# Gate stage of a fused attention and MoE kernel: the planner holds operand pieces back on VectorE and ScalarE while a PSUM bank's reading is due

## The chip, the cores and the metric

One NeuronCore of a Trainium2 chip runs the whole program. The metric is the device time of one execution in microseconds (us). The engines are TensorE (PE; its weight loads are listed as PEld), VectorE (DVE), ScalarE (ACT), GpSimd (POOL) and SyncE (SP), which here issues all DMAs. Each engine works through its own list of instructions in the order in which the program was written, and waits on semaphores where an instruction needs what another engine has made, or a buffer that another engine still reads.

## What is computed

The reference, cut to what matters:

```python
def reference(q, k, v, n_sink, window, w1, w2, w3, wo, w_in, w_out, g_ln):
    a = softmax(mask(q @ k.T / 8))            # 4 x 8 heads, 768 positions, 4 sinks, window 128
    x = (a @ v) as 3072 tokens x 512
    h = ((x @ w1) * (x @ w2)) @ w3 @ wo       # the gate is the product of the first two
    h = h @ w_in                              # 512 -> 1024
    s = h * softmax(h)
    return layer_norm(s) * g_ln @ w_out       # 3072 x 512, float32
```

## The kernel before

After attention, the rest of the program is one list of tasks. The function `op` (line 925) notes for each task its engine, an expected duration in ns, a rank, the step to run and the sets of places that it reads and writes. `arrange` (line 49) then plans the lists: it keeps a clock for each engine, puts every task whose predecessors are placed into `wait[engine]` with the time at which it becomes ready, moves it to `go[engine]` once the engine's clock has come to that time, and takes from `go` the task with the lowest rank. A rank is roughly the time in ns at which the task is wanted. An engine is free again `OVER` ns before a task ends (82 for DVE, 95 for ACT), a result of TensorE is ready for others 400 ns after its end (`PE_NS`), one of another engine after 232 ns. The order in which tasks are taken becomes the order of the program; the clock itself leaves no trace on the chip.

The gate computes a = x @ w1 and b = x @ w2 and multiplies them. Both matrix products are done as 2 x 2 block products with seven multiplications in place of eight (Strassen's scheme in Winograd's form). There are four batches (`order`, line 988), four groups of columns `m` in each, and 14 products in each group: seven (`k`) for w1 (`z` = 0) and seven for w2 (`z` = 1), in the order

```python
both = [(1, 0), (1, 1), (2, 0), (6, 0), (2, 1), (6, 1), (5, 0), (7, 0),
        (5, 1), (7, 1), (4, 0), (3, 0), (4, 1), (3, 1)]
```

A product (`product`, line 974) is six matmuls of 128x128 by 128x384, since every operand is split into a high and a low part (high by high, high by low, low by high, for two blocks of rows). It is planned with MM = 1041 ns. It is written into one PSUM bank of six, X, Y and Z for each `z` (line 971): bank index 3 z + BANK[k]. The eight banks are allocated as four tiles of two banks (`four_banks`, line 888): tile 0 holds X and Y of z = 0, tile 1 holds Z of z = 0 and X of z = 1, tile 2 holds Y and Z of z = 1. So (2,0) and (6,0) write into the same tile, and so do (2,1) and (5,0), (4,1) and (3,1), and (1,1) after (3,1).

The results are read from the banks by two kinds of instructions, the readings. A ScalarE copy (`copy`, line 940, recorded at line 158) reads Y after k = 1, 6, 7 and, for z = 0, after 4. A VectorE addition or multiplication (`two`, line 946, recorded at line 948) reads X after k = 2, Z after k = 7 and k = 3, and, for z = 1, Y after k = 4. VectorE then multiplies the two halves' results, `p_[0]*p_[1]` after (2,1), `u3[0]*u3[1]` after (7,1), `u2[0]*u2[1]` after (3,1), from SBUF to SBUF (line 948 as well), and SP sends each to DRAM (`abd`).

On the same two engines run the pieces that make operands. `parts_of` (line 952) makes the factors of a block: sums (line 368), high parts (ScalarE, line 158) and low parts (VectorE, line 365, into `hold` for x or into g). They make the factors of the next batch's x at the end of each batch, of w1's and w2's later groups in the first batch, and of the folded w3 @ wo in the last. `convert` (line 1010) turns float64 weights into float32: two ScalarE pieces, `w_sign` (VectorE, line 342), `w_high` (VectorE, line 351) and `w_c` (POOL, line 359). `ns_of` (line 162) gives a piece's planned time: for DVE 140 + 1.055 ns for each column, so 545 ns for 384 columns and 680 for 512.

After the gate come the second product (56 products of 24 matmuls, MM = 2082), the hidden layer with the norm, and the last product, all in the same task list. Their tasks on VectorE and ScalarE, such as the split of `w_in` and the first operands of the second product (`prep`), may be placed while the gate still runs.

The edit touches `RANK`, `arrange` and `op`; it works on the order of the tasks of `parts_of`, `convert`, `two` and `copy` in the gate.

Of the kernel before, what the change touches and what calls it, by code (L numbers as in the profile page):

```python
# [26 lines left out]
    mask=62.62, load=22.12, scores=-355.79, max=-67.26, exp=-12.34, total=-62.48, norm=40.89, T=-21.59,  # L27
    stay=29.46, R_T=-100.61, sink_T=-182.3, T_copy=-50.24, sink_copy=-116.03, V=51.95, out=-62.87, w_load=18.71,
    w_a=-69.73, w_b=67.42, w_c=24.26, w_hi=47.52, w_lo=3.94, fold=163.21, fold_out=40.78, parts=-92.47,
    spill=-105.5, x_parts=71.86, later=-5.34, stage=0.0,  # L30
)
WO_AT, WO_BY, W3_AT, W3_BY, W12_AT, W12_BY = -4.0, 3.0, 21.0, 3.4, 30.0, 12.0
OWN_NS, OTHER_NS, PE_NS = 19, 232, 400

OVER = dict(DVE=82, ACT=95, POOL=45)

PART_OF = dict(scores="rows", V="columns")
SWITCH = {("all", "rows"): 95, ("all", "columns"): 95, ("columns", "all"): 100, ("columns", "rows"): 100}
# [10 lines left out]
def arrange(tasks, ranks=None):  # L49


    ranks = RANK if ranks is None else ranks
    rank = [t[2] + ranks[t[3]] for t in tasks]
    last_w, readers = {}, {}
    before, follow = [0] * len(tasks), [[] for _ in tasks]
    for n, (eng, ns, s, key, f, args, r, w, after) in enumerate(tasks):
        pre = set()
        for x in r:
            if x in last_w:
                pre.add(last_w[x])  # L60
            readers.setdefault(x, []).append(n)
        for x in w:
            if x in last_w:
                pre.add(last_w[x])
            pre.update(m for m in readers.pop(x, ()) if m != n)
            last_w[x] = n
        pre.discard(n)
        before[n] = len(pre)
        for m in pre:
            follow[m].append(n)  # L70
    engine = [t[0].rstrip("+") for t in tasks]
    free = {e: 0 for e in engine}
    if "mask" in (t[3] for t in tasks):
        free["DVE"] = 4000
    port = 0
    kind = "all"
    stay = ranks.get("stay", 0.0)
    at_ns = [0] * len(tasks)
    wait, go = {e: [] for e in free}, {e: [] for e in free}
    for n, e in enumerate(engine):  # L80
        if not before[n]:
            heapq.heappush(wait[e], (0, n))
    order = []
    while len(order) < len(tasks):
        start, eng = min(
            (free[e] if go[e] else max(free[e], wait[e][0][0]), e) for e in free if go[e] or wait[e]
        )
        while wait[eng] and wait[eng][0][0] <= start:
            n = heapq.heappop(wait[eng])[1]
            heapq.heappush(go[eng], (rank[n], n))  # L90
        n = heapq.heappop(go[eng])[1]
        change = 0
        if eng == "PE":
            heapq.heappush(go[eng], (rank[n], n))
            to = {x: PART_OF.get(tasks[x[1]][3], "all") for x in go[eng]}
            x = min(go[eng], key=lambda x: (x[0] + stay * ((kind, to[x]) in SWITCH), x[1]))
            go[eng].remove(x)
            heapq.heapify(go[eng])
            n, change, kind = x[1], SWITCH.get((kind, to[x]), 0), to[x]
        if tasks[n][0][-1] == "+" and port > start:  # L100
            others = [x for x in go[eng] if tasks[x[1]][0][-1] != "+"]
            if others:
                heapq.heappush(go[eng], (rank[n], n))
                go[eng].remove(min(others))
                heapq.heapify(go[eng])
                n = min(others)[1]
            else:
                start = port
        order.append(n)
        end = start + tasks[n][1] + change  # L110
        free[eng] = max(start, end - OVER.get(eng, 0))
        if tasks[n][0][-1] == "+":
            port = free[eng]
        for m in follow[n]:
            lag = OWN_NS if engine[m] == eng else PE_NS if eng == "PE" else OTHER_NS
            at_ns[m] = max(at_ns[m], end + tasks[n][8] + lag)
            before[m] -= 1
            if not before[m]:
                heapq.heappush(wait[engine[m]], (at_ns[m], m))
    return order  # L120
# [3 lines left out]
def attention_moe_kernel(  # L124
# [27 lines left out]
    PE, DVE, ACT, POOL, SP = nc.tensor, nc.vector, nc.scalar, nc.gpsimd, nc.sync  # L152
# [24 lines left out]
    def path(stack, banded):  # L177
# [292 lines left out]
        def x_factors(b):  # L470
            x = x_t[b]
            blk = [x[:, 2 * k:2 * k + 2, S // 2 * n:S // 2 * (n + 1)] for n in range(2) for k in range(2)]
            return factors("right", blk, lambda n: (xop[:, xlie[n], 0], xop[:, xlie[n], 1]))
# [90 lines left out]
        if banded:  # L564
# [143 lines left out]
            tasks = []  # L708
# [155 lines left out]
        else:  # L864
            general_fold()
            general_attention()
            for n in range(4):
                w, m = ("w1", "w2")[n % 2], n // 2
# [20 lines left out]
        banks = {t.tensor.name for t in four_banks}  # L889
        bank = [t[:, i] for t in four_banks for i in range(2)]  # L890
# [14 lines left out]
        def toks(ap):  # L905

            name = ap.tensor.name
            if name not in grain:
                return [name]
            g = grain[name]  # L910
            if g >= P * 384:
                end = ap.offset + sum(d[0] * (d[1] - 1) for d in ap.ap)
                return {(name, x) for x in range(ap.offset // g, end // g + 1)}
            starts = [ap.offset]
            dims = [d for d in ap.ap[1:] if d[0] and d[1] > 1]
            run = 1
            if dims and dims[-1][0] == 1:
                run = dims.pop()[1]
            for stride, n in dims:
                starts = [o + stride * i for o in starts for i in range(n)]  # L920
            return {(name, x) for o in starts for x in range(o // g, (o + run - 1) // g + 1)}

        tasks = []

        def op(eng, ns, rank, outs, ins, f, *args, after=0, both=False, then=None):

            r = set().union(*(toks(a) for a in ins)) if ins else set()
            w = set().union(*(toks(a) for a in outs))
            if then is not None:
                r.add(then)  # L930
            tasks.append((eng + "+" * (eng == "POOL" or both), ns, rank, "stage", f, args, r - w, w, after))

        def dma(rank, out, in_, then=None):

# [17 lines left out]
        def parts_of(steps, cols, rank, sums="POOL", lows="DVE"):  # L952

            for kind, n, outs, ins, args in steps:
                eng = "ACT" if kind == "hi" else sums if kind == "sum" else lows[n % len(lows)] if isinstance(lows, tuple) else lows
                k = 1
                for d in outs[0].shape[1:]:
                    k *= d

                many = outs[0].shape[1]  # L960
                by = max(1, many * 512 // k) if len(outs[0].shape) > 2 else many
                for i in range(0, many, by):
                    w, r, a = ([x[:, i:i + by] if hasattr(x, "shape") else x for x in l] for l in (outs, ins, args))
                    op(eng, ns_of(eng, k * by // many), rank(n, kind), w, r, do_step, kind, engines[eng], a, both=eng == "DVE")
# [19 lines left out]
        both = [(1, 0), (1, 1), (2, 0), (6, 0), (2, 1), (6, 1), (5, 0), (7, 0), (5, 1), (7, 1), (4, 0), (3, 0), (4, 1), (3, 1)]  # L984
# [38 lines left out]
        op("SP", 475, 50000, [g_sb], [], lambda: SP.dma_start(out=g_sb, in_=g_ln.rearrange("(c p) -> p c", p=P)), after=3000)  # L1023
        MM = 1041
        later = [("win", f) for f in range(8)] + [("wout", f) for f in range(8)]
        wpiece = [slots[0][:, 4 * i * KB:4 * (i + 1) * KB] for i in range(3)]
        wfop = [t[:, 14 * KB * i:14 * KB * (i + 1)].rearrange("p (s u n) -> p s u n", s=7, u=2) for t in groups[:2] for i in range(2)]
        for bi, b in enumerate(order):
            if bi >= 2:
                dma(now - 40000, slots[b % 2], xd[b].rearrange("p c n -> p (c n)"))  # L1030
            if bi:
                parts_of(x_factors(b), 768, part_rank(1, now, MM), sums="DVE")
            for m in range(4):
                if bi == 0 and m > 1:
                    for u, w in enumerate(("w1", "w2")):
                        for i in range(2):
                            convert((w, m + 4 * i), pairs[np_ % 3][:, i], u, now - 18000 + 1000 * u)
                        parts_of(pair_factors("left", pairs[np_ % 3], group(w, groups[m])), 0, part_rank(0, now, MM))
                        np_ += 1
                if bi in (1, 2):  # L1040
                    for _ in range(2):
                        key = later.pop(0)
                        d = pairs[0][:, key[1] % 2]
                        rank = now + 20000
# [22 lines left out]
                for k, z in both:  # L1067
                    l, r = FACTORS[k]
                    bk = product(
                        k, z, now, MM, TH, [[gw[z][:, l, u, c, :] for c in range(2)] for u in range(2)],  # L1070
                        [[xop[:, xlie[r], u, c, :] for c in range(2)] for u in range(2)],
                    )
                    now += MM
                    if k in (1, 6, 7):
# [21 lines left out]
                            send(2, u2[0], now + 5000)  # L1096


        MM = 2082
        abop = [hold[:, 12 * i * KB:12 * (i + 1) * KB].rearrange("p (u c n) -> p u c n", u=2, c=4) for i in range(3)]  # L1100
        abk = [t.rearrange("p (c n) -> p c n", c=4) for t in (
# [14 lines left out]
        def prep(g):  # L1116
# [4 lines left out]
            b, k = order[bi], seq[i]  # L1121
            at_ns = base + 2 * MM * g
            b11, b12, b22, b21, spare = abk
# [21 lines left out]
        for g in range(7 * B):  # L1145
            bi, i = divmod(g, 7)
            b, k = order[bi], seq[i]
            if bi in (1, 2) and i in (0, 1, 3, 5):
                f = 4 * (bi - 1) + (0, 1, 3, 5).index(i)
# [6 lines left out]
            t = abt.pop(g)  # L1156
# [34 lines left out]
        stage = [atF(20 + 2 * i, 2) for i in range(3)]  # L1191
# [73 lines left out]
        for c in range(2 * PAIRS):  # L1265
            h, t = divmod(c, 3)
# [60 lines left out]
        for n in range(PAIRS):  # L1327
            a = lna[n % 3]
# [90 lines left out]
```

## Time and profile before

| | us |
|---|---|
| median of three runs | 927.65 (926.5 to 927.68) |
| the profiled execution, its own time | 927.59 |
| its span, first to last instruction | 925.2 |
| TensorE busy in the span | 888.6 |
| VectorE busy | 700.0 |
| ScalarE busy | 548.8 |
| GpSimd busy | 183.4 |

All times in the profile are counted from the first instruction. Attention ends at about 263 us, the gate at about 522 us, the second product at about 640 us and the hidden layer at about 815 us. The page counts an engine as busy while an instruction of its own runs. Idle time of an engine is listed with the next instruction, in brackets, with the instruction that ended the wait. A line number with an arrow, out<-in, names what an instruction writes and reads: `bank` is PSUM, `hold` and `g` are operands, `arF` and `ar` are buffers in SBUF.

### The profile page before, as it was taken

Reading aid. Unit: us, or ns where it says so; the run is one execution under the profiler, and the core shown is the slowest. Engines: PE = TensorE matmul, PEld = TensorE weight load, DVE = VectorE, ACT = ScalarE, POOL = GpSimd, SP = SyncE. Lnnn points to the kernel's source line nnn. Section 1 sums busy time; section 2 is a strip of 40 time slices with the busy share of each in tenths; the row PEclk is TensorE's granted clock in tenths of the full one; section 3 lists DMA queues with packets and bytes.
Section 4 is the critical chain, followed back from the end, with each engine's and each line's share of the span. In section 5 each row is a group of like instructions: output and inputs, shape, how many; then the busy total and the mean of one; then the engine's idle time right before and its main releaser. Section 6 shows DMA issues by size and latency. Waiting matters only on the chain.

```text
span 925.2 us, 15584 instructions
## 1 busy us (share of the span) xinstructions
PE 888.6 (96%) x5392; PEld 749.8 (81%) x5392; DVE 700.0 (76%) x1646; ACT 548.8 (59%) x1251; POOL 183.4 (20%) x243
## 2 busy tenths in 40 slices
PE   7999999999999899999998999999999999999996
PEld 3555665665579898989888999999888888999996
DVE  6988888676958786773776897794788877898761
ACT  6887877765746444752543566563667576755441
POOL 2664655451225322120000000000010011000000
PEclk9999999999999999999999999999999999999999
DMA  7566657632236367563132265443243343454411
GB/s 273 182 232 235 204 188 252 215 123 80 69 100 184 128 203 240 191 214 125 56 130 76 85 208 188 158 146 124 104 146 127 125 160 137 172 194 143 177 58 61
DMA packets 84760, 143.72 MB, mean 155 GB/s; under 512 B 6976, under 2 KB 58432, under 8 KB 82240
## 3 DMA queue, kind: packets, MB, share of 16 engines
q1 hardware_dynamic: 84672, 142.64, 46.1%
q8 instruction: 44, 0.72, 0.3%
q14 instruction: 44, 0.36, 0.1%
HBM read 95.43 MB, written 47.19 MB: 154 GB/s over the span
## 4 chain that ended last, share of the span: by engine, by line
PE 82%; DVE 12%; DMA 2%; issue 2%; ACT 1%; POOL 1%; SPq 0%; DVEq 0%; ACTq 0%; POOLq 0%
PE bank L155 56%; PE s L155 11%; PE pa L155 6%; PE pat L644 4%; DVE arF L948 3%; PE bank L1233 2%; DVE hold L365 2%; DVE g L365 2%; PE pn L656 1%; PE pn L650 1%; DVE ar L368 1%; DVE sa L600 1%; DMA arF<-in_moe_w_in_dram 1%; DVE ring L661 1%; DMA qk<-in_qk_dram 1%
## 5 line engine op out<-in xcount | busy, mean ns | idle before, releaser
L155 PE MATMUL bank<-hold,g 128*128 128x384 f32 x2016 | 360.7, 338 | 15.4 <-DVE arF L948 11.1
L155 PEld LDWEIGHTS bank<-hold,g 128*128 128x128 f32 x2016 | 349.8, 189 | 26.4 <-DVE arF L948 19.2
L155 PE MATMUL bank<-g,hold 128*128 128x512 f32 (+1 forms) x1080 | 202.2, 342 | 0.6 <-ACT ar L158 0.5
L155 PEld LDWEIGHTS bank<-g,hold 128*128 128x128 f32 x1080 | 169.2, 190 | 22.3 <-ACT ar L158 1.0
L158 ACT ACTIVATE arF<-bank 128x384 f32<-128x384 f32 (+1 forms) x160 | 80.8, 519 | 115.5 <-PE bank L155 80.5
L615 ACT ACTIVATE sa<-sa,st 128x288 f32<-128x288 f32 (+1 forms) x192 | 95.7, 501 | 20.3 <-DVE st L600 17.4
L600 DVE CUSTOM_DVE_ANT_0 sa<-s,masks 128x288 f32<-128x288 f32 (+1 forms) x192 | 76.8, 418 | 23.9 <-PE s L155 23.6
L948 DVE TENSOR_TENSOR arF<-bank,arF 128x384 f32<-128x384 f32 x96 | 53.0, 554 | 51.7 <-PE bank L155 23.4
L365 DVE TENSOR_TENSOR hold<-ar,hold 128x384 fp32r<-128x384 f32 (+2 forms) x137 | 84.6, 648 | 8.5 <-ACT hold L158 8.2
L1221 POOL TENSOR_TENSOR stt<-stt,half 128x1 f32<-128x1 f32 x24 | 17.3, 721 | 371.0 <-DVE stt L1219 363.2
L158 ACT ACTIVATE hold<-ar 128x384 fp32r<-128x384 f32 (+2 forms) x137 | 75.4, 586 | 18.0 <-DVE ar L368 13.8
L155 PE MATMUL s<-qk 64*128 64x288 f32 (+2 forms) x384 | 75.0, 439 | 8.0 <-DMA qk<-in_qk_dram 6.0
L158 ACT ACTIVATE ar<-bank 128x256 f32<-128x256 f32 (+1 forms) x80 | 33.8, 423 | 73.9 <-PE bank L155 73.5
L155 PE MATMUL bank<-g,g 128*128 128x256 f32 x504 | 66.3, 285 | 3.9 <-DVE ar L948 2.2
L661 DVE COPY ring<-pat 128x512 f32<-128x512 f32 (+1 forms) x96 | 60.9, 640 | 11.3 <-PE pat L644 10.9
L155 PEld LDWEIGHTS bank<-g,g 128*128 128x128 f32 x504 | 62.5, 192 | 5.5 <-DVE ar L948 3.0
L155 PEld LDWEIGHTS s<-qk 64*128 64x128 f32 x384 | 34.0, 193 | 35.9 <-issue 15.0
L155 PE MATMUL s<-hold 128*128 128x512 f32 x192 | 59.5, 423 | 0.0
L155 PE MATMUL pa<-ring,vn 128*64 128x256 f32 (+1 forms) x448 | 56.1, 357 | 1.5 <-DVE ring L661 1.0
L644 PE MATMUL pat<-identr,sa 128*128 128x128 f32 x352 | 56.5, 281 | 0.0
L948 DVE TENSOR_TENSOR ar<-bank,ar 128x256 f32<-128x256 f32 (+1 forms) x60 | 28.4, 475 | 32.9 <-ACT ar L158 19.1
L368 DVE TENSOR_TENSOR ar<-ar 128x256 f32<-128x256 f32 (+3 forms) x92 | 51.5, 571 | 0.8
(97 smaller groups left out, 1150.4 us busy)
## 6 DMA issues: line engine op xcount, KB each, us to landing
qk<-in_qk_dram SPq DMA_DIRECT2D x15, 1088.0 KB, 5.1
raw<-in_moe_w_dram SPq DMA_DIRECT2D x24, 512.0 KB, 5.1
abd<-arF SPq DMA_DIRECT2D x64, 192.0 KB, 2.0
lnd<-arF SPq DMA_DIRECT2D x48, 256.0 KB, 2.2
ar<-lnd SPq DMA_DIRECT2D x8, 1024.0 KB, 5.6
vn<-in_v_dram SPq DMA_DIRECT2D x16, 384.0 KB, 3.2
arF<-abd SPq DMA_DIRECT2D x8, 768.0 KB, 5.0
ar<-abd SPq DMA_DIRECT2D x8, 768.0 KB, 4.7
```

What stands on the lines that cost most here:

```text
L155: PE.matmul(o, lhsT=l, rhs=r, start=start, stop=stop, skip_group_check=True)
L158: ACT.activation(out=o, in_=i, func=AF.Copy, scale=s)
L365: eng.tensor_tensor(out=lo, in0=src, in1=fl(hi), op=ALU.subtract)
L368: eng.tensor_tensor(out=out, in0=a, in1=b, op=ALU.add if sign > 0 else ALU.subtract)
L600: DVE.tensor_tensor_reduce(out=sa[s][:, h, :n], in0=s_bank[s_at(s, h)][:, :n], in1=m_qb[j, h], op0=ALU.add, op1=ALU.min, scale=-scale, sca ...
L615: ACT.activation(out=a[:, h, :n], in_=a[:, h, :n], func=AF.Exp, scale=-1.0, bias=st_t[s][:, h:h + 1], accum_out=rs_t[p, j // 2][:, i:i + 1],)
L644: PE.transpose(pt[:, h, u, :], a[:, h, o:o + P], ident)
L650: PE.transpose(pn[0:n + 2 * SINKS, s % 2, :], a[:, 256 - n:256 + 2 * SINKS], ident)
L661: DVE.tensor_copy(out=ring[:, :, 2 * j + u0:2 * j + 2, :], in_=pat_t.pop(s)[:, :, u0:, :])
L948: eng, ns_of(eng, cols), rank, [out], [a, b], lambda: engines[eng].tensor_tensor(out=out, in0=a, in1=b, op=o),
L1221: op("POOL", 550, rank + 900, [st[7]], [st[6]], lambda: POOL.tensor_tensor(out=st[7], in0=st[6], in1=half, op=ALU.pow))
L1233: PE.transpose(bk[:, i * P:(i + 1) * P], e[:, (4 * g + i) * P:(4 * g + i + 1) * P], ident)
```

## The change

Tasks of the gate on VectorE and ScalarE get one of two new kinds in place of `stage`: `bank` if they read a PSUM bank, `gate` if not. Both have the rank offset 0.0. When the planner has picked a `gate` task on one of these engines, it looks up the earliest time `due` at which a `bank` task that is already in `wait` becomes ready, if that one's rank is less than 4000 above the picked task's. If the picked task would not be over 200 ns (`MARGIN`) ahead of `due`, the planner takes the lowest-ranked task of `go` that would; if there is none, it puts the picked task back and sets the engine's clock to `due`. Tasks made after the gate's loops keep the kind `stage`, and DMA, POOL and TensorE tasks do too.

```diff
-    spill=-105.5, x_parts=71.86, later=-5.34, stage=0.0,
+    spill=-105.5, x_parts=71.86, gate=0.0, bank=0.0, later=-5.34, stage=0.0,
 )
 OVER = dict(DVE=82, ACT=95, POOL=45)
+MARGIN = 200
...
+        if tasks[n][3] == "gate" and eng in ("DVE", "ACT"):
+
+            due = min((t for t, m in wait[eng] if tasks[m][3] == "bank" and rank[m] < rank[n] + 4000), default=None)
+            if due is not None:
+                fits = [x for x in [(rank[n], n)] + sorted(go[eng]) if start + tasks[x[1]][1] - OVER[eng] + MARGIN <= due]
+                if not fits:
+                    heapq.heappush(go[eng], (rank[n], n))
+                    free[eng] = due
+                    continue
+                if fits[0][1] != n:
+                    heapq.heappush(go[eng], (rank[n], n))
+                    go[eng].remove(fits[0])
+                    heapq.heapify(go[eng])
+                    n = fits[0][1]
...
+        gate_is_on = [True]
+
         def op(eng, ns, rank, outs, ins, f, *args, after=0, both=False, then=None):
...
-            tasks.append((eng + "+" * (eng == "POOL" or both), ns, rank, "stage", f, args, r - w, w, after))
+            kind = "stage"
+            if gate_is_on[0] and eng in ("ACT", "DVE"):
+                kind = "bank" if {a.tensor.name for a in ins} & banks else "gate"
+            tasks.append((eng + "+" * (eng == "POOL" or both), ns, rank, kind, f, args, r - w, w, after))
...
+        gate_is_on[0] = False
         MM = 2082
```

## Rows read from the trace of the kernel before

**Rows 1.** The page, part 1: busy time, share of the span, instructions.
```profile
PE 888.6 (96%) x5392; PEld 749.8 (81%) x5392; DVE 700.0 (76%) x1646; ACT 548.8 (59%) x1251; POOL 183.4 (20%) x243
```
**Rows 2.** Windows (stretch, length, busy PE, PEld, DVE, ACT, POOL, clock, DMA): gate, second product.
```profile
263.40:521.70 258.30, 243.79 (x1345) 233.49 (x1346) 180.82 (x334) 129.01 (x257) 45.98 (x40) 0.99 0.47 152
521.70:640.00 118.30, 118.30 (x680) 117.75 (x679) 97.98 (x200) 66.71 (x141) 0.00 (x0) 1.00 0.52 166
```
**Rows 3.** The chain that ended last, in order of time: start, length, what.
```profile
507.88 147.05 PE bank L155 x822
```
**Rows 4.** Waits in the gate: engine, line, releaser, us in total, times, longest.
```profile
POOL arF L359 <- DVE arF L351: 73.5, 13, 18.5
...
PE bank L155 <- DVE arF L948: 11.1, 16, 1.2
PE bank L155 <- ACT arF L158: 2.6, 4, 0.9
```
**Rows 5.** Timeline of PE in the gate: start, length; idle before it, releaser.
```profile
271.86 30.15 PE L155 MATMUL bank<-hold,g 128*128 128x384 f32 x168 [0.36 <-DVE arF L948]
...
325.24 28.51 PE L155 MATMUL bank<-hold,g 128*128 128x384 f32 x156 [0.32 <-DVE arF L948]
...
357.26 6.54 PE L155 MATMUL bank<-hold,g 128*128 128x384 f32 x36 [0.18 <-ACT arF L158]
364.28 13.84 PE L155 MATMUL bank<-hold,g 128*128 128x384 f32 x78 [0.48 <-DVE arF L948]
378.86 11.78 PE L155 MATMUL bank<-hold,g 128*128 128x384 f32 x66 [0.74 <-DVE arF L948]
391.04 3.39 PE L155 MATMUL bank<-hold,g 128*128 128x384 f32 x18 [0.40 <-DVE arF L948]
...
401.50 45.27 PE L155 MATMUL bank<-hold,g 128*128 128x384 f32 x252 [0.97 <-DVE arF L948]
447.75 9.66 PE L155 MATMUL bank<-hold,g 128*128 128x384 f32 x54 [0.98 <-DVE arF L948]
458.02 5.50 PE L155 MATMUL bank<-hold,g 128*128 128x384 f32 x30 [0.61 <-DVE arF L948]
464.02 9.63 PE L155 MATMUL bank<-hold,g 128*128 128x384 f32 x54 [0.51 <-DVE arF L948]
...
480.78 9.64 PE L155 MATMUL bank<-hold,g 128*128 128x384 f32 x54 [0.91 <-DVE arF L948]
491.16 5.48 PE L155 MATMUL bank<-hold,g 128*128 128x384 f32 x30 [0.74 <-DVE arF L948]
...
507.88 14.13 PE L155 MATMUL bank<-hold,g 128*128 128x384 f32 x79 [0.67 <-DVE arF L948]
```
**Rows 6.** Timeline of DVE ahead of PE's stop at 480.78.
```profile
477.90 0.56 DVE L948 TENSOR_TENSOR arF<-bank,arF 128x384 f32<-128x384 f32 x1 [1.09 <-PE bank L155]
478.37 1.89 DVE L365 TENSOR_TENSOR g<-ar,g 128x512 fp32r<-128x512 f32 x3
480.18 0.55 DVE L948 TENSOR_TENSOR arF<-bank,arF 128x384 f32<-128x384 f32 x1
```
**Rows 7.** Timeline of DVE ahead of PE's stop at 491.16.
```profile
489.42 0.56 DVE L948 TENSOR_TENSOR arF<-arF,bank 128x384 f32<-128x384 f32 x1 [0.73 <-PE bank L155]
489.89 0.42 DVE L368 TENSOR_TENSOR ar<-ar 128x256 f32<-128x256 f32 x1
490.22 0.42 DVE L365 TENSOR_TENSOR g<-ar,g 128x256 fp32r<-128x256 f32 x1
490.56 0.55 DVE L948 TENSOR_TENSOR arF<-bank,arF 128x384 f32<-128x384 f32 x1
```
**Rows 8.** Timeline of DVE ahead of PE's stops at 458.02 and 507.88.
```profile
456.94 0.55 DVE L948 TENSOR_TENSOR arF<-arF 128x384 f32<-128x384 f32 x1
...
506.67 0.68 DVE L365 TENSOR_TENSOR g<-arF,g 128x512 fp32r<-128x512 f32 x1
```
**Rows 9.** Timeline of DVE in the first batch, low parts of w1 and w2.
```profile
303.66 2.38 DVE L365 TENSOR_TENSOR g<-ar,g 128x512 fp32r<-128x512 f32 x2
```

## The prediction

> **What bounds the kernel now.** I read the page's busy times first, then the chain that ended last, then windows of the stage that the edit touches, and there the waits and the timelines of single engines. TensorE is busy 888.6 us of the span of 925.2 [rows 1], so only its idle time is to be had, and the question is how much of it lies in the gate and belongs to VectorE or ScalarE. The gate runs from 263.4 to 521.7 us. In those 258.3 us TensorE is busy 243.79, so 14.5 us are idle; in the next stage it is busy all of 118.30 us for 680 matmuls, 0.174 us each [rows 2]. At that pace the gate's 1344 matmuls would take 233.8 us, 24.5 less than they do: a stop costs somewhat more than its idle time. The clock in both windows is 0.99 to 1.00, so it is no part of this. From 507.88 on the chain is one piece of 147.05 us of matmuls [rows 3]: what the gate gives up reaches the end of the program, and no engine there waits to take it back. In the gate TensorE waited 16 times for VectorE's line 948, 11.1 us, and 4 times for a ScalarE copy, 2.6 us [rows 4]. Those 13.7 us are what the change can reach.
>
> **Where the stops are.** With the order of `both`, a product takes 1.04 us (six matmuls of 0.174), and each stop can be placed by counting products. They come at two places of the 14.
>
> Place A is (5,0), two products after (2,0) and (2,1) were read. At 477.90 the reading of (2,0) starts after 1.09 us of idle; three pieces of 1.89 us follow; the reading of (2,1) starts only at 480.18 [rows 6], and TensorE, idle 0.91, goes on at 480.78 [rows 5]. The reading of (2,0) waits 1.09 us although its own product has ended: it starts when (6,0), which writes the other half of the same two-bank tile, is done. In the same way (5,0) waits for the reading of (2,1), its neighbour in the second tile. So from the first reading's end to the moment that the second is ready the chip leaves 1.04 - 0.47 = 0.57 us for pieces, and whatever runs longer stops TensorE.
>
> Place B is (1,1) of the next group, which waits for the reading of (3,1). At 489.42 the reading of (4,1) starts, then two pieces (0.33 and 0.34 us until the next start), and at 490.56 the reading of (3,1) [rows 7]; TensorE stops 0.74 at 491.16 [rows 5]. Without the two pieces about 0.07 would be left.
>
> **The change, part by part.** It adds and removes no instruction and no DMA; `rank` of the two new kinds is 0.0 as before. It changes the order of VectorE's and ScalarE's lists in the gate, and by it when SP's sends and POOL's `w_c` can start.
>
> (1) *A piece with a higher rank than the reading.* The planner holds it back when it would end less than 200 ns before the reading is due. At due time the reading has the lower rank and goes first. This is the working case. Operand pieces for the next batch, conversions of `w_in` and `w_out`, and the fold's factors at the end of the gate rank some 2,000 to 50,000 above the readings beside them, since they are due so many ns later.
>
> Place B: both pieces go behind the reading. At 491.16 (0.74 [rows 5]), and one group earlier with the same figures, I take 0.6 each of the 0.67 that two pieces last [rows 7]; at 378.86 (0.74) one 512-column conversion piece, 0.6 as each of the three of rows 6; at 364.28 (0.48) a short one of 0.33 as in rows 7. Sum 2.1 us.
>
> Place A: here the plan's window is longer than the chip's. The plan holds the two readings 2 x 1041 ns apart; minus the reading's 463 (545 less the overlap of 82) and the margin of 200 that leaves 1419 ns: three pieces of 384 columns (3 x 463 = 1389) fit, or two of 512 columns (598 each). So of the four pieces ahead of 401.50 (0.97) and 447.75 (0.98) one goes, 0.47 each, which is the step of a 384-column instruction at 477.90 [rows 6]; of the three 512-column pieces ahead of 480.78 (0.91) one goes, 0.6, and so one group later with the same figures; the three ahead of 464.02 (0.51) stay. The stop at 271.86 (0.36) goes, since its one conversion piece is 0.6 long. Sum 2.5 us.
>
> Four stops with a single or last piece that doesn't fit end altogether: 271.86, counted already, and 325.24, 357.26 and 391.04 with 0.32, 0.18 and 0.40 [rows 5], 0.9 us. Where a stop ends altogether I add 0.2 us for what matmuls lose around it (the 24.5 above against 14.5 idle, over some twenty stops, give 0.5 at most): 4 x 0.2 = 0.8.
>
> Gain of (1): 2.1 + 2.5 + 0.9 + 0.8 = 6.3 us. Its ends: nothing, if every piece is replaced by one that just fits, and 11.1 + 2.6 = 13.7 [rows 4], if no stop is left.
>
> (2) *A piece with a lower rank than the reading, by less than 4000.* The test looks at readings that still wait. At due time the reading is no longer in `wait`, the piece has the lower rank, and it goes first after all: the plan idles, the order on the chip is the old one. So it is with the product `u3[0]*u3[1]` (rank 10 x 1041 + 5000 = 15410) against the reading of (3,1) (14 x 1041 + 1000 = 15574): the piece at 456.94 [rows 8] stays, and with it the 0.61 at 458.02 [rows 5] and one like it in the batch before. Worth nothing, and it costs nothing on the chip, which does not wait for the plan's clock.
>
> (3) *What isn't held back.* Pieces created after the gate keep the kind `stage`. The split at 506.67 [rows 8] makes (1,1) stop for 0.67 at 507.88 [rows 5], and stays. Stops in which a reading waits for TensorE or for a DMA have no piece to move. Nothing.
>
> (4) *The pieces that go later.* Each waits for one reading (0.47) and for that reading's own wait, up to 1.09 [rows 6], so 0.5 to 1.6 us. In the last batch nobody waits for them for tens of us: the second stage needs the fold's factors after 521. In the first batch they are needed at once: at 303.66 two splits into g last 2.38 us [rows 9] just ahead of the products that read them. A product of two partial results that goes later sends later: one reading, 0.47, on SP's queue, and the next copy into that tile may wait for it. `w_c` on POOL starts later too, but POOL waited 73.5 us for these in all [rows 4], so it hides that. The trace of before has no such delay to read a price from. From below nothing; from above one full 1.56 us at each batch's start and in each of the first batch's two late groups, six in all, 9.4. I take one full delay, 1.5, since most such pieces are pushed by a reading that was due anyway.
>
> Sum: 6.3 - 1.5 = 4.8 us. The profiled execution took 927.59 us (span 925.2), 0.06 under the median, so the forecast against either is 927.6 - 4.8 = 922.8 us.
>
> **Rivals.** *No order changes that matter.* If most pieces ahead of readings rank below them, (2) is the whole story and the time stays at 927 or 928. The rows speak against it: the pieces from 473 to 497 us serve a stage that begins over 24 us later. *Slower: the moved pieces become the wait.* In the first batch TensorE's own order was planned around late operands, and at each batch's start VectorE is nearly full. From four delays of 1.56 us (6.2) the gain is gone; at the upper end, six, the time is 927.6 - 6.3 + 9.4 = 930.7. For it speaks the row at 303.66; against it the 4000 in the rule, which lets urgent pieces pass. *The stops move.* Pieces taken out of place B fall into place A's window, whose plan lets three through where the chip has time for one; then the 2.1 of B are lost again, and 925 is left.
>
> *A reading held by its own bank alone.* Then the readings of (2,0) would start at their product's end, VectorE would keep the plan's window, and with the pieces held back every stop for line 948 would go: 927.6 - 11.1 = 916.5 [rows 4]. The 1.09 us of rows 6 speak against it. The Trainium skill's page PSUM — Partial Sum Buffer, in its summary of rules for kernel authors, says that a reader beside a running matmul has only to be in a different bank; the trace disagrees for this program, whose waits join both banks of a tile.
>
> **How the numbers follow.** A difference of 0.2%, 1.9 us, is about what a measurement of this kernel can tell from no change. The forecast, faster by 3 to 9 us, has 0.55; the stops move (925), 0.13; a bank alone (916.5), 0.06; no order that matters, 0.14; slower (930.7), 0.12. Faster is 0.55 + 0.13 + 0.06 = 0.74. The forecast's own range is 919 to 925. For 8 in 10 the range must reach 925 and most of the unchanged case above, and the forecast's better end below: 917.5 to 928.5.
>
> **What would show it.** TensorE's stops at (1,1) in the last batch fall from 0.74 to under 0.2, with the readings of (4,1) and (3,1) back to back on VectorE; stops at (5,0) shrink to 0.3 to 0.5 but stay; the 0.61 at the batch starts and the 0.67 at the end of the gate are still there; the gate shrinks from 258.3 us to about 253.5, and VectorE is idle longer ahead of readings. I am wrong if TensorE waits for lines 365 or 158 into hold or g for over 2 us, if the two stops of the last batch at (1,1) stay, or if the gate shrinks and a later stage takes it back.

## The result, and the profile after

The changed kernel takes 917.88 us, median of four runs (916.59 to 918.6), beside 927.08 us for four runs of the kernel before (924.66 to 927.68): the ratio is 0.9904, interval 0.9882 to 0.9926. The direction was forecast and the range holds the time, but the gain is 9.2 us where 4.8 were forecast. The profiled execution took 916.59 us, 11.0 less than the profiled one of before.

The page of the kernel after, part 1, as in [rows 1]:

```profile
PE 883.6 (97%) x5392; PEld 748.6 (82%) x5392; DVE 695.7 (76%) x1646; ACT 547.3 (60%) x1251; POOL 183.1 (20%) x243
```

Its windows of the gate and of the second product, columns as in [rows 2]:

```profile
263.60:511.40 247.80, 239.09 (x1344) 232.47 (x1345) 175.99 (x333) 128.42 (x257) 45.71 (x40) 1.00 0.49 158
511.40:629.70 118.30, 118.30 (x681) 117.99 (x681) 98.45 (x201) 66.27 (x141) 0.00 (x0) 1.00 0.51 167
```

The same work is done by the same number of instructions. The gate went from 258.3 to 247.8 us [rows 2], the span from 925.2 to 914.7: all 10.5 us came out of the gate, and in the second product (56 products of 12 matmuls each) TensorE is busy throughout, as before. The end of the chain of waits shows that nothing took it back:

```profile
483.10 12.79 PE bank L170 x72
497.59 146.82 PE bank L170 x822
```

The second line is the long piece of [rows 3], 10.3 us earlier. Not all of the 10.5 is the change's. The window of the gate's first stretch in the kernel before:

```profile
263.40:267.20 3.80, 3.80 (x13) 3.80 (x14) 0.00 (x0) 0.49 (x1) 0.00 (x0) 0.55 0.70 224
```

The same stretch in the kernel after:

```profile
263.60:267.20 3.60, 3.58 (x21) 3.59 (x22) 0.00 (x0) 0.98 (x2) 0.00 (x0) 1.00 0.68 211
```

Before, 13 matmuls filled 3.80 us at a granted clock of 0.55; after, 21 took 3.58 at 1.00. By the starts of the products this is worth 1.6 us: the first three take 4.82 us before and 3.23 after. It isn't the edit's: TensorE's order is the same there, and the profiled executions of the kernels below show both, with the edit and without it.

The waits in the gate (as in [rows 4]):

```profile
PE bank L170 <- DVE arF L968: 5.4, 10, 0.7
...
PE bank L170 <- DVE g L380: 1.6, 1, 1.6
...
PE bank L170 <- ACT arF L173: 1.0, 2, 0.8
```

Line 968 is line 948 of before, 173 is 158, 380 is 365, 383 is 368 and 170 is 155; in the kernels below the numbers shift again, and the names beside them tell which line it is. Stops for a VectorE reading or multiplication fell from 16 and 11.1 us to 10 and 5.4. And the timeline of TensorE (as in [rows 5]):

```profile
315.08 11.37 PE L170 MATMUL bank<-hold,g 128*128 128x384 f32 x64 [1.57 <-DVE g L380]
327.06 22.59 PE L170 MATMUL bank<-hold,g 128*128 128x384 f32 x126 [0.61 <-DVE arF L968]
350.43 8.62 PE L170 MATMUL bank<-hold,g 128*128 128x384 f32 x48 [0.78 <-ACT arF L173]
359.53 13.80 PE L170 MATMUL bank<-hold,g 128*128 128x384 f32 x78 [0.47 <-DVE arF L968]
373.94 14.86 PE L170 MATMUL bank<-hold,g 128*128 128x384 f32 x84 [0.61 <-DVE arF L968]
389.40 16.97 PE L170 MATMUL bank<-hold,g 128*128 128x384 f32 x96 [0.61 <-DVE arF L968]
406.85 33.70 PE L170 MATMUL bank<-hold,g 128*128 128x384 f32 x186 [0.47 <-DVE arF L968]
441.05 9.66 PE L170 MATMUL bank<-hold,g 128*128 128x384 f32 x54 [0.51 <-DVE arF L968]
451.32 16.95 PE L170 MATMUL bank<-hold,g 128*128 128x384 f32 x96 [0.61 <-DVE arF L968]
468.68 14.02 PE L170 MATMUL bank<-hold,g 128*128 128x384 f32 x78 [0.41 <-DVE arF L968]
483.10 13.82 PE L170 MATMUL bank<-hold,g 128*128 128x384 f32 x78 [0.41 <-DVE arF L968]
497.59 22.64 PE L170 MATMUL bank<-hold,g 128*128 128x384 f32 x128 [0.67 <-DVE arF L968]
```

Count the products between two stops (1.04 us each). From 451.32 TensorE runs 16 products without a stop, where before it stopped at the sixth, (5,0), for 0.51, after 458.02. Of the ten stops for line 968, nine are at (1,1); one is left at (5,0), at 441.05.

But counting also shows what had not been expected: *TensorE's own order is another.* Set beside the order of before, 90 of the gate's 224 products stand elsewhere, from the sixteenth on. The last batch began before with (1,0) (1,1) (2,0) (6,0) (2,1) (6,1) (5,0) (7,0), and begins now with (1,0) (1,1) (2,0) (2,1) (5,0) (5,1) (6,0) (6,1). The planner places TensorE's tasks by the times at which their operands are ready in its plan; the rule makes pieces later there, and other products come first. For (6,0) of the last batch `arrange`, run on the tasks of the two kernels, has the last low part of the operand ready at 180.7 us of its own clock before and at 183.3 after, so three other products pass it. VectorE's timeline shows what that does at the two products that share a tile:

```profile
453.78 0.56 DVE L968 TENSOR_TENSOR arF<-bank,arF 128x384 f32<-128x384 f32 x1
454.26 1.49 DVE L380 TENSOR_TENSOR hold<-ar,hold 128x384 fp32r<-128x384 f32 x3
455.79 0.56 DVE L968 TENSOR_TENSOR arF<-bank,arF 128x384 f32<-128x384 f32 x1
...
481.69 0.55 DVE L968 TENSOR_TENSOR arF<-arF,bank 128x384 f32<-128x384 f32 x1 [1.19 <-PE bank L170]
482.16 0.42 DVE L383 TENSOR_TENSOR ar<-ar 128x256 f32<-128x256 f32 x1
482.49 0.55 DVE L968 TENSOR_TENSOR arF<-bank,arF 128x384 f32<-128x384 f32 x1
```

The reading of (2,0) starts at 453.78, 0.27 us after its product's end, since (6,0) now comes only after three other products; three pieces follow, and the reading of (2,1) starts at 455.79. (5,0) had started at 454.55, straight behind (2,1), ahead of that reading in the program: no stop, with three pieces between the readings as before. At 481.69 the reading of (4,1) still waits 1.19 us for (3,1), the other half of its tile, and one short piece still stands between it and the reading of (3,1): (1,1) stops for 0.41 at 483.10, where [rows 7] had two pieces and 0.74.

### The profile page after: what moved, and what is told of

It reads as the page before. It is cut to its first block, busy times and chain, and to the rows that moved or that the text cites. A ratio compares the mean times of both kernels' runs of the same rounds, so it can differ in the third digit from the quotient of the medians.

```text
span 914.7 us, 15584 instructions
## 1 busy us (share of the span) xinstructions
PE 883.6 (97%) x5392; PEld 748.6 (82%) x5392; DVE 695.7 (76%) x1646; ACT 547.3 (60%) x1251; POOL 183.1 (20%) x243
## 4 chain that ended last, share of the span: by engine, by line
PE 85%; DVE 9%; DMA 2%; issue 1%; ACT 1%; SPq 0%; POOL 0%; DVEq 0%; ACTq 0%
PE bank L170 61%; PE s L170 11%; PE pa L170 5%; PE pat L659 4%; PE bank L1254 2%; DVE arF L968 2%; PE pn L671 1%; DMA abd<-arF 1%; PE pn L665 1%; DVE sa L615 1%; DVE hold L380 1%; DVE ring L676 1%; DVE g L380 1%; DMA qk<-in_qk_dram 1%; DVE ar L383 1%
## 5 line engine op out<-in xcount | busy, mean ns | idle before, releaser
L170 PE MATMUL bank<-hold,g 128*128 128x384 f32 x2016 | 355.7, 336 | 9.6 <-DVE arF L968 5.4
L380 DVE TENSOR_TENSOR hold<-ar,hold 128x384 fp32r<-128x384 f32 (+2 forms) x137 | 82.5, 636 | 8.6 <-ACT hold L173 8.3
L1242 POOL TENSOR_TENSOR stt<-stt,half 128x1 f32<-128x1 f32 x24 | 17.3, 720 | 348.5 <-DVE stt L1240 340.7
L173 ACT ACTIVATE hold<-ar 128x384 fp32r<-128x384 f32 (+2 forms) x137 | 75.8, 586 | 17.9 <-DVE ar L383 10.3
```

The lines of the kernel that those rows point to most:

```text
L170: PE.matmul(o, lhsT=l, rhs=r, start=start, stop=stop, skip_group_check=True)
L173: ACT.activation(out=o, in_=i, func=AF.Copy, scale=s)
L380: eng.tensor_tensor(out=lo, in0=src, in1=fl(hi), op=ALU.subtract)
L1242: op("POOL", 550, rank + 900, [st[7]], [st[6]], lambda: POOL.tensor_tensor(out=st[7], in0=st[6], in1=half, op=ALU.pow))
```

## The experiments

For all of them I use one more figure, worked out from the starts of the 224 products in each trace: the time beyond 1.041 us for each (the time beyond, for short), without the first three (the clock above), for the first batch and for the other three. For the kernel before it is 6.2 + 17.3 = 23.4 us, after 3.2 + 11.3 = 14.5; the difference, 8.9, is what 0.9904 says of 927 us. Each ratio is to runs of the kernel before on the same chip.

**Two orders, taken apart.** The first run keeps the rule and holds TensorE's 224 products to the order of before (`PIN`, below, is that order; `then` makes each product wait in the plan for the one ahead of it); the second has no rule and holds them to the order of after. In both the planner lays VectorE's and ScalarE's lists for the given order, so they aren't word for word the lists of before or after (in the first, 212 of VectorE's 938 tasks in this list stand elsewhere than after).

```diff
+PIN = [...]
...
+    then = {}
+    if "mask" not in (t[3] for t in tasks):
+        ids = [n for n, e in enumerate(engine) if e == "PE"]
+        for a, b in zip(PIN, PIN[1:]):
+            then[ids[a]] = ids[b]
+            before[ids[b]] += 1
...
+        if n in then:
+            m = then[n]
+            at_ns[m] = max(at_ns[m], end)
+            before[m] -= 1
+            if not before[m]:
+                heapq.heappush(wait["PE"], (at_ns[m], m))
```

> The changed kernel, but in the gate TensorE's 224 products are pinned to the order that they have in the kernel before; VectorE's and ScalarE's lists follow the new rule. Theory LISTS (the gain lies in VectorE's and ScalarE's lists, my sizes were only too small): 917.9 +- 1.5 us, the stops of TensorE in the gate sum to about 8 us as in the changed kernel. Theory PE ORDER (about half of the gain comes from TensorE's own order, which the planner chose anew): about 922.5 us; the stops at (5,0) of some 0.3 to 0.6 us are back, the first batch has its stops of about 1 us.

> The kernel before, without the rule, but TensorE's 224 products of the gate are pinned to the order that they have in the changed kernel. Theory LISTS: no gain, 926 to 928 us. Theory PE ORDER: 921 to 923 us; the stops at (5,0) of the last two batches (0.5 to 1.0 us each before) are gone, those at (1,1) of 0.6 to 0.75 us are still there.

The rule with the old order: 924.99 us, ratio 0.9982 (0.9965 to 0.9998). The new order without the rule: 925.6, ratio 0.9981 (0.996 to 1.0002). Neither is the gain, and their sum, 0.4%, isn't either. By the products' starts the time beyond is 23.5 us in the first and 21.5 in the second, against 23.4 before. TensorE's timeline of the first (rule, old order):

```profile
306.15 19.59 PE L184 MATMUL bank<-hold,g 128*128 128x384 f32 x94 [2.53 <-DVE g L394]
...
399.18 12.91 PE L184 MATMUL bank<-hold,g 128*128 128x384 f32 x72 [0.72 <-DVE arF L982]
```

The two stops show two prices of the late pieces. Operands of the first batch come late (its time beyond goes from 6.2 to 9.4). And (6,0) is a new place, at 399.18: with its own operand late, the plan starts (6,0) some 3 us after (2,0) in place of 1.04, behind the reading of (2,0) in the program, and since the two banks are in one tile, (6,0) waits on the chip for that reading. The later batches gain 3.2 us and the first loses them. Of the second (new order, no rule):

```profile
458.32 16.97 PE L169 MATMUL bank<-hold,g 128*128 128x384 f32 x96 [0.61 <-DVE arF L962]
476.04 14.06 PE L169 MATMUL bank<-hold,g 128*128 128x384 f32 x78 [0.74 <-DVE arF L962]
490.84 14.01 PE L169 MATMUL bank<-hold,g 128*128 128x384 f32 x78 [0.74 <-DVE arF L962]
```

There is no stop at (5,0) in the last batch, so those went by the order, even without the rule (the 0.97 at the end of the batch before is still there, at 448.08); 0.74 at (1,1), whose pieces nothing holds back; and the time beyond of the first batch is 8.1.

**The rule in a part of the batches.** One line at the top of the batch loop, for the first batch alone (`bi == 0`) or for the three others:

```diff
         for bi, b in enumerate(order):
+            gate_is_on[0] = bi > 0
```

> The changed kernel with the rule for tasks made in the first batch alone. Theory REPLAN (the rule lets the planner choose a TensorE order that fits the operands' times better, which is worth some 3 us in the first batch): 922 to 924.5 us. Theory LATE PIECES (term 4 of the prediction: held-back pieces cost the first batch time): 926.5 to 930 us.

> The changed kernel with the rule for tasks made in the second to fourth batch alone. If the parts add up: about 6 us of the 9 are here, 920 to 922 us. If the whole gain hangs on the first batch's plan: 925 to 927 us. If the first batch's rule costs time: under 917 us.

First batch alone: 926.05, ratio 0.9993 (0.9977 to 1.0009); that batch gains 3.5 and the later ones, where no rule acts, lose 2.2; TensorE's order differs there too, in 38 products. The three others alone: 917.86, ratio 0.9905 (0.988 to 0.993): the whole gain, with the first batch at 6.3, as before, and 8.4 in the others in place of 17.3. Here TensorE's order differs in 58 products, none in the first two batches. In the timeline of the second, 43 products run without a stop from 362.07, where before there were four stops, from 378.86 to 401.50 (three of them in [rows 5]):

```profile
362.07 45.77 PE L170 MATMUL bank<-hold,g 128*128 128x384 f32 x258 [0.48 <-DVE arF L968]
408.32 33.37 PE L170 MATMUL bank<-hold,g 128*128 128x384 f32 x186 [0.47 <-DVE arF L968]
```

So the rule isn't needed in the first batch, and the two orders can be taken apart once more without its late operands: that kernel with TensorE held to the order of before, and the kernel before held to that kernel's order (the diff above, another list).

> The rule for tasks of the second to fourth batch alone (that run took 917.9 us), and in addition TensorE's products of the gate pinned to the order of the kernel before. Theory LISTS ALONE: 917 to 919.5 us, nothing is lost. Theory BOTH NEEDED (the rule makes operands of (6,0) and others late at a batch's start; TensorE's new order hides that and spares the stops at (5,0)): 921 to 924 us, with new stops at (6,0) of about 0.7 us at each batch's start.

> No rule, but TensorE's products pinned to the order that the run with the rule in the later batches has (58 of 224 products stand elsewhere than before, all in the third and fourth batch). Theory LISTS ALONE: 926 to 928 us. Theory BOTH NEEDED: 922 to 925 us; the stops at (5,0) of the third and fourth batch are gone, those at (1,1) stay at 0.6 to 0.75 us.

They take 925.76, ratio 0.9985 (0.9969 to 1.0001), and 926.28, ratio 0.9986 (0.997 to 1.0002). Again neither alone, and this time without a late operand in the first batch (its time beyond is 6.3 and 6.2). TensorE's timeline of the first (rule, old order):

```profile
395.11 50.17 PE L184 MATMUL bank<-hold,g 128*128 128x384 f32 x270 [1.95 <-DVE arF L982]
...
459.14 11.03 PE L184 MATMUL bank<-hold,g 128*128 128x384 f32 x61 [0.72 <-DVE arF L982]
```

VectorE's timeline of the same kernel, ahead of the stop at 395.11:

```profile
392.63 1.02 DVE L394 TENSOR_TENSOR hold<-ar,hold 128x384 fp32r<-128x384 f32 x2
393.56 0.55 DVE L982 TENSOR_TENSOR arF<-arF 128x384 f32<-128x384 f32 x1
394.03 0.55 DVE L397 TENSOR_TENSOR ar<-ar 128x384 f32<-128x384 f32 x1
394.50 0.55 DVE L982 TENSOR_TENSOR arF<-bank,arF 128x384 f32<-128x384 f32 x1
```

(6,0) waits 1.95 for the reading at 394.50, the one of (2,0), ahead of which the plan still has four other instructions; all (6,0) of the later batches cost 3.0 us. TensorE's timeline of the second (new order, no rule):

```profile
411.09 7.06 PE L169 MATMUL bank<-hold,g 128*128 128x384 f32 x30 [2.16 <-DVE arF L962]
```

VectorE's timeline of the same kernel, ahead of this stop of (1,1):

```profile
408.00 0.55 DVE L962 TENSOR_TENSOR arF<-arF,bank 128x384 f32<-128x384 f32 x1 [1.02 <-PE bank L169]
409.35 0.43 DVE L356 TENSOR_SCALAR arF<-arF 128x512 int32<-128x512 int32 x1 [0.79 <-DMA woutd<-arF]
409.88 0.69 DVE L365 SCALAR_TENSOR_TENSOR arF<-arF 128x512 int32<-128x512 int32 x1
410.49 0.55 DVE L962 TENSOR_TENSOR arF<-bank,arF 128x384 f32<-128x384 f32 x1
```

Between two readings that the chip makes ready together stand two conversion pieces, the first of which waits 0.79 for a DMA. The kernel with the rule from the second batch on has its stop of 0.47, at 408.32 above, at this place:

```profile
407.38 0.42 DVE L357 TENSOR_SCALAR arF<-arF 128x512 int32<-128x512 int32 x1
407.71 0.55 DVE L968 TENSOR_TENSOR arF<-bank,arF 128x384 f32<-128x384 f32 x1
408.18 0.68 DVE L366 SCALAR_TENSOR_TENSOR arF<-arF 128x512 int32<-128x512 int32 x1
```

The rule puts the second piece behind the reading; the first fits its margin and stays. So 0.6 of the 2.16 is what the rule forbids, and 0.79 is a wait for a DMA that doesn't show there and that no part of the rule looks at. The waits for line 948 by its new numbers, all in one table (us, times):

| | order of before | order that the rule brings |
|---|---|---|
| no rule | 11.1, 16 | 8.3, 13 |
| rule | 8.4, 14 | 5.4, 10 |
| no rule, order of the later-batches kernel | | 10.1, 13 |
| rule from the second batch on | 9.3, 13 | 5.4, 10 |

Lists and order were chosen together by one plan, and each without the other gives back most of the gain, in the first batch or at (6,0) and (1,1). What these four kernels can't show is either part in its pure form, since a held order makes the planner lay other lists.

**What is left at (1,1).** Two runs try to sharpen the rule. In the first, a reading that is ready goes ahead of a piece that ranks lower by less than 4000 (case 2 of the prediction):

```diff
+            ready = [x for x in go[eng] if tasks[x[1]][3] == "bank" and x[0] < rank[n] + 4000]
+            if ready:
...
+                n = min(ready)[1]
-            if due is not None:
+            elif due is not None:
```

> The changed kernel, with one addition to the planner: where a reading is already ready (in go) and ranks less than 4000 above the picked gate piece, the reading goes first. The multiplication of u3 then comes after the reading of (3,1). If the stops of 0.61 us (four of them, at (1,1)) are due to that one multiplication between two readings: they fall to about 0.14, 4 x 0.47 = 1.9 us less, about 916.0 us. If the planner's shifts of TensorE's order matter as much as the lists: anything from 914 to 920 us, with stops at other places.

919.31, ratio 0.9913 (0.9893 to 0.9933): no better than the change. The four stops of 0.61 fell to 0.14, as meant, but the time beyond at (7,0) rose from 1.1 to 3.1 in the three later batches, and that of the first batch from 3.2 to 5.3. One of the stops at (7,0):

```profile
413.40 23.59 PE L176 MATMUL bank<-hold,g 128*128 128x384 f32 x132 [1.20 <-ACT arF L179]
```

The second is the kernel with the rule from the second batch on and a margin of 500 ns in place of 200:

```diff
-MARGIN = 200
+MARGIN = 500
```

> The rule for the second to fourth batch alone, with a margin of 500 ns in place of 200. My term for the stops at (1,1) assumed that no piece is left between the two readings ahead of them; with 200 ns one short piece still fits. If that is all: the stops of 0.41 us at (1,1) of the last batch fall to 0.14, some 1 us less in all, about 917 us. If a longer margin makes operands late: over 919 us, with stops at other products.

923.19, ratio 0.9936 (0.9913 to 0.9958), beside 0.9905 (0.988 to 0.993) with the smaller margin: by the ratios a third of the gain is lost, though the two intervals overlap. The time beyond says the same, 18.7 us against 14.7. The last batch does what was meant:

```profile
356.26 24.69 PE L170 MATMUL bank<-hold,g 128*128 128x384 f32 x138 [0.96 <-ACT arF L173]
...
458.04 57.13 PE L170 MATMUL bank<-hold,g 128*128 128x384 f32 x318 [0.61 <-DVE arF L968]
```

The two stops of 0.41 are gone (53 products without a stop from 458.04), but TensorE's order moved again, to 110 places other than before where the smaller margin has 58, and new stops stand elsewhere, such as the 0.96 of (2,0) at 356.26. The margin can't be sized by one place alone.

**The wait behind the stops.** Most stops for readings come at two banks of one tile, where a reading waits for the product in the other half. The planner knows nothing of these waits: its sets of places count PSUM in steps of one bank (`grain`, 512), so it holds a reading to be due by its own product's end. These kernels leave the lists alone and give the six banks other places in the four tiles: first with both X in one tile, both Z in one and each Y in a tile of its own (`[0, 2, 4, 1, 6, 5]`, with the rule); then X with Z of the same `z` and each Y alone, without the rule and with it.

```diff
+        where = [0, 4, 1, 2, 6, 3]
...
-            b = bank[3 * z + BANK[k]][:, 0:width]
+            b = bank[where[3 * z + BANK[k]]][:, 0:width]
...
+        where[:] = range(6)
```

> The changed kernel; in the gate the six banks are spread differently over the four two-bank tiles: both X in one tile, both Z in one, each Y alone. The lists of all engines stay as they are, only the waits between banks of one tile change. If waits join both banks of a tile (as the 1.09 us idle ahead of the reading of (2,0) suggests): that idle time is gone, the stops at (1,1) (ten, 5.4 us) mostly vanish, and the time falls to 911 to 914 us. If the wait has another cause: 917.9 us, stops unchanged.

> The kernel before, all lists as they are; in the gate only the six banks lie differently in the two-bank tiles: X with Z of the same z in one tile, each Y alone, so that no bank shares a tile with one that is written in the next two products. If the stops of the kernel before come from waits that join the two banks of a tile: those at (5,0) and (1,1) go, and the time falls by 8 to 12 us to 915 to 918.5 us with no rule at all; VectorE's reading of (2,0) no longer idles 1.09 us. If they come from pieces ahead of readings alone: the reading is as late as before, 925 to 927.5 us.

> The changed kernel with the same placing of banks as in the run above, lists unchanged. If the waits between the banks of a tile are what is left of the stops at (1,1): from 917.9 to 909 to 912.5 us. If the rule and the placing remove the same stops: not under 914 us, and within 2 us of the kernel before with this placing.

The first takes 916.22, ratio 0.9879 (0.986 to 0.9898), less of a gain than expected. No stop is left at (1,1), but (3,0) and (3,1) now share a tile, and (3,1) stops for the reading of (3,0):

```profile
452.14 43.98 PE L170 MATMUL bank<-hold,g 128*128 128x384 f32 x252 [1.20 <-DVE arF L968]
496.86 14.89 PE L170 MATMUL bank<-hold,g 128*128 128x384 f32 x84 [0.74 <-DVE arF L968]
```

The second is the kernel *before*, with the orders of TensorE, VectorE and ScalarE the same task by task, and other places: 908.18, ratio 0.9802 (0.9777 to 0.9826), about twice the gain expected. Its time beyond is 6.2 us in place of 23.4. TensorE's timeline:

```profile
366.72 153.50 PE L155 MATMUL bank<-hold,g 128*128 128x384 f32 x884 [1.03 <-ACT arF L158]
```

And VectorE's:

```profile
464.93 0.55 DVE L948 TENSOR_TENSOR arF<-bank,arF 128x384 f32<-128x384 f32 x1
465.39 1.89 DVE L365 TENSOR_TENSOR g<-ar,g 128x512 fp32r<-128x512 f32 x3
467.20 0.55 DVE L948 TENSOR_TENSOR arF<-bank,arF 128x384 f32<-128x384 f32 x1
```

These are the instructions of [rows 6], some 13 us earlier: the same three pieces between the same two readings, but the 1.09 us of idle time ahead of the first is gone, and TensorE runs on through 884 matmuls without a stop. The third, the kernel after with these places, takes 907.58, ratio 0.9794 (0.9767 to 0.982), time beyond 3.9. The two intervals overlap almost wholly: with the waits across a tile gone, the rule is worth nothing that these runs can tell, and either kernel is faster than the kernel before and the kernel after of this case.

## Why the prediction was right and wrong

**What bounds, and where it would show: right.** The gain came out of TensorE's idle time in the gate, reached the end whole, and later stages took nothing back. Two readings beside it were off. The clock is said to be no part of it, but the mean of 0.99 hides the first 3.8 us at 0.55, 1.6 us of the 24.5. And 13.7 us were taken as all that the change could reach; the time beyond is 23.4, and other places for the banks took 17.2 of it.

**The step that failed is the opening one of "The change, part by part".** It says that the change "changes the order of VectorE's and ScalarE's lists in the gate, and by it when SP's sends and POOL's `w_c` can start", and all four steps then keep TensorE's order fixed. The planner makes one plan for all engines, and TensorE's order in it came out different in 90 products. The forecast's own scene, the rule under the old order, was run twice: 0.9982 with the rule in all batches and 0.9985 without the first, a gain of 1.7 and 1.4 us, not 4.8; the products' starts leave even less, 23.5 and 23.0 us beyond against 23.4. The gain of 9 is that of lists and order together. That the range, from 917.5 up, holds 917.88 is luck: its better end allowed for a larger gain of the same steps, not for another order.

**Step 1, place A: the gain is there, by another way.** The forecast was one piece fewer at each (5,0), 2.5 us, with stops that shrink and stay. One did just that, 447.75 with 0.98 to 441.05 with 0.51; the others ended. The time beyond at (5,0) in the three later batches went from 5.4 to 1.0 us. The new order without the rule leaves 2.1, the rule under the old order 1.9: each alone does most of it, and the forecast's own scene gave 3.5, more than the 2.5 forecast. The four stops that were to end altogether are not in the list of after either.

**Step 1, place B: mis-sized.** It put both pieces behind the reading, to be left with under 0.2. Place A's own arithmetic, used here, says otherwise: the plan holds the readings of (4,1) and (3,1) 1041 ns apart; less 463 and the margin of 200, 378 are left, and a piece of 256 columns steps by 328. So one goes and one stays: 0.41, as measured at 468.68 and 483.10. With other stops at (1,1) taking turns (406.85 is new), (1,1) has 7.3 us beyond in the three later batches, as against 7.1 before: nothing in place of 2.1.

**Step 2 and step 3: right.** The 0.61 at 451.32, the one like it in the batch before (389.40) and the 0.67 at 497.59 stand as forecast. Of two more of 0.61, the one at 327.06 is new and the one at 373.94 was 0.74.

**Step 4: the price is real, and mis-sized, in the scene that didn't come.** Under the old order the late pieces cost the first batch 3.2 us (a stop of 2.53 at 306.15) and made (6,0) wait, 1.8 us in the later batches: 5.0 in place of 1.5. With the new order that batch gained 3.0 instead; one stop of 1.57 for a late g at 315.08 is left.

**The rivals.** *Slower* is not what happened, but its price is that of step 4, and without another order it eats most of the gain: the rule under the old order is the nearest thing to it that was run. *The stops move* came true for the 2.1 us of place B, but they moved among the (1,1), not into place A. *A bank alone* gave 916.5, near the measured 917.88 by chance, since its mechanism isn't there: the reading of (4,1) still waits 1.19 us for the other half of its tile. Its idea was the better guide all the same: where a neighbour bank no longer holds a reading up, the time is 908.18 without any rule. The Trainium skill's PSUM — Partial Sum Buffer, summary of rules for kernel authors, says that a reader beside a running matmul has only to be in another bank. The runs agree where it is read as what the work needs: the kernel before gains 2% by places alone. They disagree where it is read as what this program waits for: its waits join the two banks of a tile.

**What stays open.** Why the plan's two choices help each other is shown place by place ((6,0), (1,1), the first batch's operands), not as a rule: another plan could bring other pairs. Whether the old lists, word for word, would gain anything under the new order was not run. The stop of 0.78 at 350.43, for a ScalarE copy, was not followed further.

## What to carry to other kernels

Where one planner lays all engines' lists, a rule on two of them can move the third: before sizing its stops one by one, make the plan's other orders part of the forecast, or hold them fixed and say so. A planner's window has to be checked against the chip's at every place by the same arithmetic, as a piece that just fits the margin can still stop TensorE (0.41 us at (1,1)). And before pieces are held back from a wait, ask why the wait is there: here pairing other banks in the tiles was worth 2%, twice what the scheduling rule brought, and left the rule nothing that the runs could tell. The planner counted PSUM by banks while the program's waits go by tiles of two.

## What the runs showed of the hardware

The granted clock in the first 3.8 us of the gate was 0.55 in some profiled executions (13 matmuls in 3.80 us) and 1.00 in others (21 in 3.58), near the lower and at the higher of its two levels, 1.2 and 2.4 GHz. Ahead of it stood the same in the kernels before and after: attention's last small matmuls and a stop of 0.91 us. It is worth 1.6 us of an execution, nearly the 0.2% at which runs of this kernel are told apart, so two traces alone would have given the edit that much too much. It doesn't follow the edit: of the two kernels with the rule, the same lists and other places of the banks, the first had the loss (4.83 us for the first three products) and the second had not (3.23).
